# A fused attention and two-MLP kernel: where the last 16 weight blocks are turned from 64-bit words into floats, and the order of a quad's seven products

## The chip, the cores and the metric

The kernel runs on one core of one Trainium2 chip. The metric is the device time of one execution in microseconds (us). Before the change three runs took 874.74, 876.16 and 879.68 us; the median is 876.16 us.

## The reference

All inputs are 64-bit floats, the output is 32-bit. Cut to what matters:

```python
# attention: 4 batches, 8 heads, 576 positions, head size 64, causal window of 64
attn = softmax(masked(q @ k.T / 8)) @ v          # -> x, 2304 tokens x 512
# first MLP
h = (x @ w1) * (x @ w2) @ w3                     # 512 -> 1024 -> 1024
x = h @ w_out                                    # 1024 -> 512
# second MLP
h = x @ w_in                                     # 512 -> 2048
out = maximum(0.01 * h, h) @ w_out2              # 2048 -> 512
```

The weight `moe2_w_out` of the last line is called `w_out2` in the kernel, `moe2_w_in` is `w_in`.

## The kernel before, in words

**Arithmetic.** Each matmul operand is split into a high part (fp32r) and a low part, and `mm3` (lines 74 to 77) adds three matmuls, high x high, high x low and low x high. ACT writes the high part, DVE subtracts to get the low part.

**Words.** A weight arrives as 64-bit words, 128x512 of them (512 KB) to a *unit*. `advance` (line 283) moves a pipeline of units on by one step at each call: one unit is scaled by ACT (line 292), and DVE does three operations per unit, a mask-and-or (line 306), a shift (line 313) and an or (line 317); then `fin` uses the 128x512 float block `f`. A unit passes its stages in four successive calls, and a new call can start the next one. `load_unit` (line 273) issues the load of the raw words on SP into one of four `raw` buffers; `feed` loads ahead as far as the buffers allow. The blocks `f` also have four buffers (tag "f"), and both tags are shared with other uses: `w_ops` takes two `f` and one `raw`, `y_ops` four `f` and two `raw`, `load_w` one `f`.

The first 40 units (w3, w_out, w1, w2) are used at once. The next 32 (16 of `w_in`, 16 of `w_out2`) are only converted and stored as floats into the DRAM tile `wd` (`keep`, line 381), to be read back later. Before the change all 32 are converted beside the first MLP, from batch 2 on: one or two calls of `advance` per step of the loop at line 629 (lines 636 to 638).

**Stages in order of time.** Attention of a batch runs beside the first MLP of the batch before it.
- *x to y*: for each of 4 batches 16 steps (two token halves, eight blocks f). `ab_step` computes two products in PSUM (tag "ab"); ACT copies one of them (line 495), DVE multiplies (line 500) and splits. `y_step`, two steps later, accumulates y in four PSUM banks with w3 @ w_out already multiplied together. y goes to the DRAM tile `yd`.
- *y to h*: 24 *quads*. Each is a 2x2 block product by a seven-product scheme (`class Quad`, line 585): w side p of 0 to 7 (`NF`), token side c of 0 to 2 (`NP`). Each product is six matmuls of 128x384 into a PSUM bank (tag "pr"); there are eight banks, two in the pool `ps_h` and six in `ps2`. ACT copies the first product of a quad (line 606), DVE adds the others to partial sums (line 608, seven adds a quad), and SP stores four results per quad to the DRAM tile `hd`. `w_ops(p)` reads floats of `w_in` back from `wd` and makes seven sums and splits; `y_ops(c, j)` does that for y. For c = 2 the low parts of y are made by GpSimd (POOL) instead of DVE. The quads' order (line 741): p = 0 to 2 for c = 0, 1 and 2 (quads 0 to 8), then p = 3 to 7, each for c = 0 to 2 (quads 9 to 23).
- *h to out*: `o_step`, 6 token blocks x 16 blocks of h. `load_w` and `split_w` bring `w_out2`'s floats from `wd`, `load_h` and `split_h` the blocks of h. `ahead` issues them some steps early; the first four calls stand behind quad 21.

**Order of the work.** A planner replays the program with a model of each instruction's duration and writes a fixed order for each engine. An instruction that was written earlier in the program has priority; `first()` (line 70) lifts what stands in it by 3000 places. `tc.issue_after(ins)` makes the instructions in its block stand behind `ins` on the same engine. On the chip each engine then keeps the planned order, whatever the times turn out to be. The quads' products carry no such tie, so the planner can put a product of a later quad ahead of one of an earlier quad when a `ps_h` bank is free and a `ps2` bank isn't; it can also put quad 0's first two products (in `ps_h`) between the last steps of x to y.

**Loads at the seam.** `early` (line 656) holds `w_ops(0)`, `y_ops(0, 0)` and `y_ops(0, 1)`. The first is called at step 2 of the last batch, the other two only when all 32 units are through (line 639) or behind the loop (lines 657 to 659).

Of the kernel before, what the change touches and what calls it, by code (L numbers as in the profile page):

```python
# [21 lines left out]
def tile_kernel(ctx: ExitStack, tc: tile.TileContext, q, k, v, w1, w2, w3, w_out, w_in, w_out2, out):  # L22
# [16 lines left out]
    B, H, S, D = q.shape  # L39
# [34 lines left out]
    def mm3(ps, lh, ll, rh, rl, first, last):  # L74
        pe.matmul(ps, lhsT=lh, rhs=rh, start=first, stop=False)  # L75
        pe.matmul(ps, lhsT=lh, rhs=rl, start=False, stop=False)  # L76
        return pe.matmul(ps, lhsT=ll, rhs=rh, start=False, stop=last).ins  # L77
# [185 lines left out]
    units = []  # L263
    last = {}
    slots = {}
    n_of = {"load": 0, "scale": 0, "shift": 0, "bits": 0, "fin": 0}

    def feed():

        while n_of["load"] < min(len(units), n_of["bits"] + RAW):  # L270
            load_unit()

    def load_unit():
# [9 lines left out]
    def advance(stop):  # L283

        now = dict(n_of)
        if now["scale"] < min(stop, now["load"]):
            u = units[now["scale"]]
            w = flat(u["raw"]).bitcast(I32).rearrange("p (m two) -> p m two", two=2)
            u["lo"], u["hi"] = w[:, :, 0], w[:, :, 1]
            u["f"] = stage.tile([P, UC], F32, name="f", tag="f", bufs=4)  # L290
            with tc.issue_after(pss["copy"]) if now["scale"] >= PHASE_B else nullcontext():
                act.mul(u["f"], u["hi"].bitcast(F32), 2.0 ** -112)  # L292
                if now["scale"] < PHASE_B:
                    u["low"] = stage.tile([P, UC], I32, name="low", tag="low", bufs=1)
                    act.activation(out=u["low"], in_=flat(u["raw"]).bitcast(U8).rearrange("p (m e) -> p m e", e=8)[:, :, 3],
                                   func=AF.Copy, scale=1.0 / 32, bias=-31.0 / 64)
            n_of["scale"] += 1
        if now["fin"] < now["bits"]:
            u = units[now["fin"]]
            u["fin"](u["f"])  # L300
            n_of["fin"] += 1
        d = now["bits"] < now["shift"]
        if d:
            u = units[now["bits"]]
            f = u["f"].bitcast(I32)
            dve.scalar_tensor_tensor(out=f, in0=u["hi"], scalar=-0x80000000, in1=f, op0=ALU.bitwise_and, op1=ALU.bitwise_or)
        if now["shift"] < now["scale"]:
            u2 = units[now["shift"]]
            g = u2["f"].bitcast(I32)
            if "low" in u2:  # L310
                dve.scalar_tensor_tensor(out=g, in0=g, scalar=3, in1=u2["low"], op0=ALU.logical_shift_left, op1=ALU.bitwise_or)
            else:
                dve.tensor_scalar(g, g, 3, 0x7FFFFFF8, op0=ALU.logical_shift_left, op1=ALU.bitwise_and)
            n_of["shift"] += 1
        if d:
            if "low" not in u:
                dve.scalar_tensor_tensor(out=f, in0=u["lo"], scalar=29, in1=f, op0=ALU.logical_shift_right, op1=ALU.bitwise_or)
            n_of["bits"] += 1
            feed()

    def until(n, stop):
        while n_of["fin"] < n:
            advance(stop)
# [57 lines left out]
    def keep(i):  # L381

        return lambda f: sp.dma_start(wd[i], f)

    for p in range(NF):
        for h in range(2):
            unit(w_in[2 * P * h:2 * P * h + 2 * P, 2 * P * p:2 * P * p + 2 * P].rearrange("(k p) m -> p k m", p=P),
                 keep(2 * p + h), ("win", p, h))
    for f in range(KF2):
        unit(w_out2[P * f:P * f + P, :], keep(KF2 + f), ("wo2", f))  # L390
    KEPT = len(units)
    for name, p in [("wo", i) for i in range(4)] + [(n, p) for p in range(2) for n in ("w1", "w2")] + [("wf", i) for i in range(4)]:
        slots[name, p] = wslot((name, p))

# [112 lines left out]
    def y_step(b, hf, i):  # L507
        w = rows2(slots["wf", i // 2])
        for j in range(KD):
            if i == 0:  # L510
                yps[j] = ps_mm.tile([P, DM], F32, name="mm", tag="mm")
            ws = slice(P * j, P * j + P)
            mm3(yps[j][:, 0:NH], w[:, 0, i % 2, ws], w[:, 1, i % 2, ws], ab[i][:, 0], ab[i][:, 1], i == 0, i == KF - 1)
        if i == KF - 1:
            for j in range(KD):
                y = stage.tile([P, DM], F32, name="io", tag="io", bufs=2)[:, 0:NH]
                t0 = b * S + hf * NH
                with first():
                    act.copy(y, yps[j][:, 0:NH])
                    act.dma_start(yd[:, j, t0:t0 + NH], y)  # L520
# [64 lines left out]
    class Quad:  # L585
# [4 lines left out]
        def product(self, m):  # L590
            n_of["bank"] += 1
            pool = ps_h if n_of["bank"] % 8 in (1, 2) else ps2
            ps = pool.tile([P, DM], F32, name="pr")[:, 0:NB2]
            a, b = PRODUCTS[m]
            w, y = wop[self.p][a], yop[self.c]
            for j in range(2):
                ws = slice(P * j, P * j + P)
                pss["last"] = mm3(ps, w[:, 0, ws], w[:, 1, ws], y[:, b, j, 0], y[:, b, j, 1], j == 0, j == 1)
            return ps

        def add(self, to, ps, of):

            if to not in self.sb:
                self.sb[to] = ph.tile([P, NB2], F32, name="c", tag="c", bufs=8)
            if of is None:
                act.copy(self.sb[to], ps)
            else:
                dve.tensor_tensor(out=self.sb[to], in0=ps, in1=self.sb[of], op=ALU.add)  # L608

        def out(self, n):  # L610
            fh, th = int(n[1]) - 1, int(n[2]) - 1
            t0 = (2 * self.c + th) * NB2
            sp.dma_start(hd[:, 2 * self.p + fh, t0:t0 + NB2], self.sb.pop(n))

        def step(self, k):
            m, adds, done = ((1, [("c11", None)], []), (6, [("c12", "c11")], []), (2, [("c11", "c11")], ["c11"]),
# [9 lines left out]
    for b in range(B):  # L626
        if b + 1 < B:
            plan_att(b + 1, *((10, 26) if b == 0 else (1, 37)))
        for s in range(2 * KF):
            hf, f = divmod(s, KF)  # L630
            if b == 0:
                if hf == 0:
                    until(max(last[n, f // 2] for n in ("w1", "w2")), PHASE_B)
                for _ in range(2):
                    advance(PHASE_B)
            if 2 * KF * b + s >= 2 * KF * (B - 2) + 4:
                for _ in range(2 if b == B - 1 and s < 8 else 1):
                    advance(KEPT)
            if b == B - 1 and (s == 2 or n_of["fin"] == KEPT and len(early) > 0):
                early.pop(0)()  # L640
            ab_step(b, hf, f, 0)
            slot()
            ab_step(b, hf, f, 1)
            slot()
            ysteps.append((b, hf, f))
            if len(ysteps) > YLAG:
                y_step(*ysteps.pop(0))
            slot()
        if b == B - 2:
            att.release()  # L650
            xa.release()
            ps_at.release()
            ps_h = tc.alloc_tile_pool(name="ps_h", bufs=2, space=PSUM, side="right", reuse_waits="tile")
            yb0 = tc.alloc_tile_pool(name="yb0", bufs=1, side="right", reuse_waits="tile")
            yop[0] = yb0.tile([P, 7, 2, 2, NB2], F32R, name="yop")
            early = [lambda: w_ops(0), lambda: y_ops(0, 0), lambda: y_ops(0, 1)]
    until(KEPT, KEPT)
    for f in early:
        f()
    for e in ysteps:  # L660
        y_step(*e)

# [81 lines left out]
    for i, q in enumerate(quads):  # L744
        for k in range(7):
            with first():
                q.step(k)
            if k == 0 and order[i] == (NF - 1, 0):
                for f in range(WLEAD):
                    load_w(f)  # L750
            if k == 0 and i < FIRST * (NP - 1) and i % FIRST == 0:
                c = i // FIRST + 1
                yop[c] = ph.tile([P, 7, 2, 2, NB2], F32R, name=f"yop{c}", bufs=1)
            if k == 3:
                if i == 0:
                    w_ops(2)
                elif i < FIRST * (NP - 1) and i % FIRST in (1, 2):
                    y_ops(i // FIRST + 1, i % FIRST - 1)
                p = order[i][0] + 2 if order[i][1] == NP - 1 else 0
                if FIRST <= p < NF:  # L760
                    w_ops(p)
        if order[i] == (NF - 1, 0):
            yb0.release()
            po1 = tc.alloc_tile_pool(name="po1", bufs=4, side="right", reuse_waits="tile")
            for n in range(LOADS):
                ahead(n)
# [40 lines left out]
```

## Time and profile before

| what | value |
|---|---|
| median of 3 runs | 876.16 us |
| the profiled execution | 876.7 us, of which the span from first to last instruction is 874.9 us |
| PE (matmul) busy | 824.2 us, 94% of the span |
| DVE busy | 572.9 us, 65% |
| ACT busy | 391.0 us, 45% |
| POOL busy | 60.4 us, 7% |
| mean granted TensorE clock | 0.986 of full speed |
| last matmul of x to y ends | about 475.2 us |
| last product of y to h ends | about 663.7 us |
| first matmul of h to out starts | 666.35 us |

PE is busy nearly all the time, so the places of interest are the few where it isn't, and the ones where its clock is at the lower level. Busy shares are averages over stages with different limits; a table by stage is among the rows below.

### The profile page before, as it was taken

How to read it: one execution, taken by the hardware profiler on the slowest of the kernel's cores; microseconds unless marked ns; L12 is line 12 of the kernel's file. 1: busy time of each engine (PE TensorE's matmuls, PEld its weight loads, DVE VectorE, ACT ScalarE, POOL GpSimd, SP SyncE). 2: the span in 40 equal slices, each digit the busy share in tenths (PEclk: the TensorE clock that was granted, in tenths of full speed). 3: DMA queues.
4: the chain of work that ended last, by engine and by line, in shares of the span. 5: the costliest groups of instructions: out<-in, count | busy, mean ns of one | idle time of the engine just before them, and what ended most of it. 6: DMA issues, size and time to landing. Idle time of an engine off the chain costs nothing.

```text
span 874.9 us, 15295 instructions
## 1 busy us (share of the span) xinstructions
PE 824.2 (94%) x5332; PEld 754.2 (86%) x5332; DVE 572.9 (65%) x1435; ACT 391.0 (45%) x988; POOL 60.4 (7%) x75
## 2 busy tenths in 40 slices
PE   4789799999999999999998899999997999999997
PEld 3577699899999999999888899999996888888885
DVE  6799897554555377767775986565658555555552
ACT  6687883433343344435354421111125545555552
POOL 1012011110111011100000340000000000000000
PEclk9999999999999999999999999999998999999999
DMA  7798778763556267877962554343447335344341
GB/s 240 200 214 230 209 188 202 164 148 92 119 122 138 59 171 197 246 239 245 281 204 62 161 184 163 103 154 112 151 152 228 106 93 155 107 135 128 100 127 45
DMA packets 203693, 139.44 MB, mean 159 GB/s; under 512 B 137312, under 2 KB 181856, under 8 KB 203616
## 3 DMA queue, kind: packets, MB, share of 16 engines
q1 hardware_dynamic: 199008, 133.74, 54.3%
q10 hardware_dynamic: 4608, 4.72, 1.6%
q8 instruction: 42, 0.69, 0.3%
q14 instruction: 35, 0.29, 0.1%
HBM read 94.63 MB, written 43.78 MB: 158 GB/s over the span
## 4 chain that ended last, share of the span: by engine, by line
PE 66%; DMA 14%; DVE 11%; ACT 5%; issue 2%; SPq 1%; POOL 0%; ACTq 0%; DVEq 0%; POOLq 0%
PE o L75 8%; PE o L76 8%; PE o L77 8%; PE ab L75 6%; PE ab L76 5%; PE ab L77 5%; PE pr L75 5%; PE pr L76 5%; PE pr L77 5%; DMA raw<-in_moe_w_out_dram 3%; PE mm L75 3%; DMA raw<-in_moe_w_dram 3%; PE mm L77 3%; PE sc L175 2%; PE mm L76 2%
## 5 line engine op out<-in xcount | busy, mean ns | idle before, releaser
L75 PE MATMUL ab<-x,w 128*128 128x288 f32 x512 | 154.5, 302 | 5.2 <-ACT x L235 2.6
L76 PE MATMUL ab<-x,w 128*128 128x288 f32 x512 | 151.9, 297 | 0.0
L77 PE MATMUL ab<-x,w 128*128 128x288 f32 x512 | 151.4, 296 | 0.0
L75 PE MATMUL o<-w,g 128*128 128x512 f32 x288 | 114.5, 397 | 2.7 <-DVE c L608 2.7
L608 DVE TENSOR_TENSOR c<-pr,c 128x384 f32<-128x384 f32 x168 | 84.3, 549 | 46.1 <-PE pr L77 27.4
L76 PE MATMUL o<-w,g 128*128 128x512 f32 x288 | 114.2, 396 | 0.0
L75 PE MATMUL pr<-yop,w 128*128 128x384 f32 x324 | 100.5, 343 | 8.8 <-DVE c L608 6.4
L75 PEld LDWEIGHTS ab<-x,w 128*128 128x128 f32 x512 | 96.8, 189 | 8.1 <-ACT x L235 2.8
L76 PE MATMUL pr<-yop,w 128*128 128x384 f32 x324 | 98.9, 339 | 1.4 <-DVE yop L542 1.4
L76 PEld LDWEIGHTS ab<-x,w 128*128 128x128 f32 x512 | 96.8, 189 | 0.2
L77 PEld LDWEIGHTS ab<-x,w 128*128 128x128 f32 x512 | 96.8, 189 | 0.0
L77 PE MATMUL pr<-yop,w 128*128 128x384 f32 x324 | 96.1, 340 | 0.0
L696 DVE TENSOR_TENSOR t<-h,t 128x384 f32<-128x384 f32 x96 | 53.5, 558 | 50.5 <-ACT t L695 50.5
L77 PE MATMUL o<-w,g 128*128 128x512 f32 x288 | 84.0, 396 | 0.0
L695 ACT ACTIVATE t<-h 128x384 f32<-128x384 f32 x96 | 50.4, 525 | 56.9 <-DVE g L698 56.1
L77 PE MATMUL mm<-ab,wf 128*128 128x288 f32 x256 | 74.8, 295 | 0.0
L75 PE MATMUL mm<-ab,wf 128*128 128x288 f32 x256 | 74.6, 308 | 0.0
L76 PE MATMUL mm<-ab,wf 128*128 128x288 f32 x256 | 74.3, 293 | 0.0
L698 DVE TENSOR_TENSOR g<-t,g 128x384 fp32r<-128x384 f32 x96 | 53.5, 557 | 28.6 <-ACT g L697 28.1
L75 PEld LDWEIGHTS pr<-yop,w 128*128 128x128 f32 x324 | 60.7, 190 | 12.3 <-DVE c L608 9.4
L75 PEld LDWEIGHTS o<-w,g 128*128 128x128 f32 x288 | 54.8, 190 | 15.4 <-issue 3.0
L292 ACT ACTIVATE f<-raw 128x512 f32<-128x512 f32 x72 | 48.6, 677 | 42.3 <-DMA raw<-in_moe_w_out_dram 23.7
(99 smaller groups left out, 1505.7 us busy)
## 6 DMA issues: line engine op xcount, KB each, us to landing
hd<-c SPq DMA_DIRECT2D x96, 192.0 KB, 2.2
h<-hd SPq DMA_DIRECT2D x96, 192.0 KB, 2.4
raw<-in_moe_w_dram SPq DMA_DIRECT2D x32, 512.0 KB, 4.5
raw<-in_moe_w_out_dram SPq DMA_DIRECT2D x24, 512.0 KB, 5.2
raw<-in_moe_w_in_dram SPq DMA_DIRECT2D x16, 512.0 KB, 4.9
wd<-f SPq DMA_DIRECT2D x32, 256.0 KB, 4.6
f<-wd SPq DMA_DIRECT2D x32, 256.0 KB, 3.2
vt<-in_v_dram SPq DMA_DIRECT2D x56, 128.0 KB, 2.7
```

The costliest lines, as they stand in the source:

```text
L75: pe.matmul(ps, lhsT=lh, rhs=rh, start=first, stop=False)
L76: pe.matmul(ps, lhsT=lh, rhs=rl, start=False, stop=False)
L77: return pe.matmul(ps, lhsT=ll, rhs=rh, start=False, stop=last).ins
L175: pe.matmul(sc[:, t, :], lhsT=qb[:, t, :], rhs=kT[n][:, k0:k0 + P], start=True, stop=True)
L292: act.mul(u["f"], u["hi"].bitcast(F32), 2.0 ** -112)
L608: dve.tensor_tensor(out=self.sb[to], in0=ps, in1=self.sb[of], op=ALU.add)
L695: act.mul(t, h, 0.01)
L696: dve.tensor_tensor(out=t, in0=h, in1=t, op=ALU.max)
L698: dve.tensor_tensor(out=g[:, 1], in0=t, in1=f32(g[:, 0]), op=ALU.subtract)
```

## The change: the edits and the diff

- `n_of` gets `cap` and `room`. `feed` loads units only up to `cap`. While x to y runs, `cap` and `KEPT` end behind `w_in`'s 16 units, so `w_out2`'s 16 aren't touched there.
- In the loop of x to y `advance` is called once per step in place of once or twice; `y_ops(0, 0)` and `y_ops(0, 1)` are called at steps 8 and 11 of the last batch. The `until(KEPT, KEPT)` behind the loop goes.
- From quad 6 on, at the second and fifth product of each quad: the first such call raises `cap`, sets `room` to 3 raw buffers and loads; each later one is an `advance`, until all units are through. The scaling on ACT is tied behind the last copy of a quad's first product, the loads on SP behind the last store of a quad's result.
- Each product of a quad is tied behind the product before it on PE, the very first behind the last `y_step`.
- `load_w(0)` to `load_w(2)` are called at the fourth product of quad 20, within `first()`, in place of behind the first product of quad 21.

```diff
-    n_of = {"load": 0, "scale": 0, "shift": 0, "bits": 0, "fin": 0}
+    n_of = {"cap": 0, "room": RAW, "load": 0, "scale": 0, "shift": 0, "bits": 0, "fin": 0}
...
-        while n_of["load"] < min(len(units), n_of["bits"] + RAW):
+        while n_of["load"] < min(n_of["cap"], n_of["bits"] + n_of["room"]):
             load_unit()
...
+    n_of["cap"] = KEPT = len(units)
     for f in range(KF2):
         unit(w_out2[P * f:P * f + P, :], keep(KF2 + f), ("wo2", f))
-    KEPT = len(units)
...
-            mm3(yps[j][:, 0:NH], w[:, 0, i % 2, ws], w[:, 1, i % 2, ws], ab[i][:, 0], ab[i][:, 1], i == 0, i == KF - 1)
+            pss["pr"] = mm3(yps[j][:, 0:NH], w[:, 0, i % 2, ws], w[:, 1, i % 2, ws], ab[i][:, 0], ab[i][:, 1], i == 0, i == KF - 1)
...
-            for j in range(2):
-                ws = slice(P * j, P * j + P)
-                pss["last"] = mm3(ps, w[:, 0, ws], w[:, 1, ws], y[:, b, j, 0], y[:, b, j, 1], j == 0, j == 1)
+            with tc.issue_after(pss["pr"]):
+                for j in range(2):
+                    ws = slice(P * j, P * j + P)
+                    pss["pr"] = mm3(ps, w[:, 0, ws], w[:, 1, ws], y[:, b, j, 0], y[:, b, j, 1], j == 0, j == 1)
...
-                act.copy(self.sb[to], ps)
+                pss["copy"] = act.copy(self.sb[to], ps).ins
...
-            sp.dma_start(hd[:, 2 * self.p + fh, t0:t0 + NB2], self.sb.pop(n))
+            pss["store"] = sp.dma_start(hd[:, 2 * self.p + fh, t0:t0 + NB2], self.sb.pop(n)).ins
...
             if 2 * KF * b + s >= 2 * KF * (B - 2) + 4:
-                for _ in range(2 if b == B - 1 and s < 8 else 1):
-                    advance(KEPT)
-            if b == B - 1 and (s == 2 or n_of["fin"] == KEPT and len(early) > 0):
+                advance(KEPT)
+            if b == B - 1 and s in (2, 8, 11):
                 early.pop(0)()
...
-    until(KEPT, KEPT)
-    for f in early:
-        f()
...
-            if k == 0 and order[i] == (NF - 1, 0):
-                for f in range(WLEAD):
-                    load_w(f)
+            if k == 3 and order[i] == (NF - 2, NP - 1):
+                with first():
+                    for f in range(WLEAD):
+                        load_w(f)
+            if k in (1, 4) and i >= FIRST * (NP - 1) and n_of["fin"] < len(units):
+                if n_of["cap"] == KEPT:
+                    n_of["cap"], n_of["room"] = len(units), 3
+                    feed()
+                else:
+                    advance(len(units))
```

## Rows read from the trace of the kernel before

**Rows 1.** Busy time by stretch: length, busy us (instructions), PEclk, DMA share, GB/s.

```profile
398.00:475.20 77.20, 73.15 (x534) 71.20 (x532) 52.12 (x111) 30.83 (x69) 0.00 (x0) 1.00 0.63 199
475.20:526.20 51.00, 46.09 (x239) 44.63 (x240) 45.52 (x84) 20.27 (x44) 16.15 (x14) 0.93 0.54 168
526.20:599.60 73.40, 72.64 (x415) 72.32 (x415) 44.90 (x94) 12.44 (x25) 0.00 (x0) 1.00 0.39 130
599.60:648.60 49.00, 48.28 (x275) 47.65 (x275) 27.62 (x57) 6.00 (x14) 0.00 (x0) 1.00 0.39 132
648.60:666.30 17.70, 13.00 (x72) 12.04 (x70) 15.28 (x30) 9.81 (x19) 0.00 (x0) 0.98 0.88 281
```

**Rows 2.** PE's waits, 400 to 670 us: us in total, times, longest.

```profile
PE pr L75 <- DVE c L608: 6.4, 6, 2.1
PE pr L76 <- DVE yop L542: 1.4, 1, 1.4
PE ab L75 <- DVE p L500: 1.3, 2, 0.8
PE ab L75 <- ACT a L495: 0.9, 2, 0.5
```

**Rows 3.** PE's timeline, 475 to 668 us, five of its waits: start, us, [idle before].

```profile
477.08 0.44 PE L75 MATMUL pr<-yop,w 128*128 128x384 f32 x1 [1.88 <-ACT w L573]
...
493.61 0.44 PE L75 MATMUL pr<-yop,w 128*128 128x384 f32 x1 [0.83 <-DVE c L608]
...
503.61 0.45 PE L75 MATMUL pr<-yop,w 128*128 128x384 f32 x1 [2.10 <-DVE c L608]
...
658.81 0.45 PE L75 MATMUL pr<-yop,w 128*128 128x384 f32 x1 [1.95 <-DVE c L608]
...
666.35 0.77 PE L75 MATMUL o<-w,g 128*128 128x512 f32 x1 [2.69 <-DVE c L608]
```

**Rows 4.** Busy time of five slices of 5 us, for the clock behind the waits.

```profile
475.00:480.00 5.00, 3.12 (x12) 2.70 (x11) 3.76 (x8) 4.42 (x11) 0.00 (x0) 0.77 0.42 125
480.00:485.00 5.00, 5.00 (x27) 5.00 (x26) 3.53 (x7) 2.67 (x7) 0.00 (x0) 0.89 0.65 193
505.00:510.00 5.00, 5.00 (x22) 5.00 (x21) 4.22 (x9) 1.02 (x2) 2.10 (x2) 0.66 0.97 307
665.00:670.00 5.00, 3.65 (x9) 2.91 (x10) 2.98 (x7) 0.77 (x2) 0.00 (x0) 0.54 0.95 322
670.00:675.00 5.00, 5.00 (x19) 4.03 (x18) 4.55 (x8) 4.09 (x8) 0.00 (x0) 0.77 0.51 162
```

**Rows 5.** Groups by line, whole span: count | busy us, mean ns | idle before.

```profile
L608 DVE TENSOR_TENSOR c<-pr,c 128x384 f32<-128x384 f32 x168 | 84.3, 549 | 46.1 <-PE pr L77 27.4 <-ACT c L606 16.8 <-issue 0.5
L306 DVE SCALAR_TENSOR_TENSOR f<-raw,f 128x512 int32<-128x512 int32 x72 | 49.2, 684 | 0.7
L292 ACT ACTIVATE f<-raw 128x512 f32<-128x512 f32 x72 | 48.6, 677 | 42.3 <-DMA raw<-in_moe_w_out_dram 23.7 <-DMA raw<-in_moe_w_dram 15.0 <-DVE nm L179 1.7
L317 DVE SCALAR_TENSOR_TENSOR f<-raw,f 128x512 int32<-128x512 int32 x32 | 23.7, 741 | 0.1
L313 DVE TENSOR_SCALAR f<-f 128x512 int32<-128x512 int32 x32 | 13.5, 421 | 18.1 <-ACT f L292 17.9
```

**Rows 6.** DVE's timeline, 636 to 644 us.

```profile
640.28 4.06 DVE L608 TENSOR_TENSOR c<-pr,c 128x384 f32<-128x384 f32 x8 [8.00 <-ACT c L606]
```

**Rows 7.** DVE's timeline, 650 to 660 us.

```profile
656.05 0.69 DVE L260 TENSOR_TENSOR w<-f,w 128x512 fp32r<-128x512 f32 x1 [2.11 <-ACT w L259]
```

**Rows 8.** ACT's timeline, 650 to 660 us.

```profile
655.40 0.62 ACT L259 CAST w<-f 128x512 fp32r<-128x512 f32 x1 [2.04 <-DMA f<-wd]
```

**Rows 9.** Instructions on tile f: duration ns min/median/max, first to last start.

```profile
L679 SPq DMA_DIRECT2D f<-wd x16: 319/320/1330, 586.7 to 671.2; - x16
```

**Rows 10.** ACT's waits, 314 to 446 us, where w_in's and w_out2's units are converted.

```profile
ACT f L292 <- DMA raw<-in_moe_w_out_dram: 18.0, 11, 3.5
```

**Rows 11.** The page's DMA issues: count, KB each, us to landing.

```profile
raw<-in_moe_w_out_dram SPq DMA_DIRECT2D x24, 512.0 KB, 5.2
```

## The prediction, made before the changed kernel ran

> **What bounds the kernel now.** I read the busy time by stretch first [rows 1]. PE is the bound: in the two middle stretches of y to h it is busy 72.6 of 73.4 us and 48.3 of 49.0. DVE is the second: 45.5 of 51.0 us in quads 0 to 5, where it splits y and w beside the quads' additions, but 44.9 of 73.4 and 27.6 of 49.0 after that. So work on DVE is nearly free from quad 6 on and dear before it. Then PE's waits [rows 2], which show that between 400 and 670 us PE stood still for DVE's additions (6.4 us), for early products whose y wasn't split yet (1.4 us) and for a and b, held up by conversions (1.3 and 0.9 us). The timeline gives five of these their places [rows 3]: the seam from y to the quads (1.88 us), two in quads 0 to 5 (0.83 and 2.10 us), the last quads (1.95 us) and the first `o` (2.69 us). Last the clock: where PE had stood still it came back at the lower of its two levels, 1.2 in place of 2.4 GHz, for a while [rows 4]. Behind the seam the two slices lose 5 x 0.23 + 5 x 0.11 = 1.7 us, behind the wait at 503.6 us 5 x 0.34 = 1.7 us, and around 666 us 5 x 0.46 + 5 x 0.23 = 3.4 us, of which some 0.3 us fell on the wait itself, so 3.1 us. The wait at 658.8 us has no drop of its own size behind it: the 17.7 us stretch stands at 0.98 [rows 1].
>
> PE's floor in the quads is 72.64 us / 415 = 0.175 us a matmul [rows 1], 1.05 us a product and 7.35 us a quad.
>
> **The change part by part.** I work against the profiled execution, 876.7 us with 1.8 us outside its span of 874.9. It is 0.5 us above the median of 876.16, and that is taken off at the end.
>
> *The 16 units leave x to y.* Each costs DVE 684 + 421 + 741 = 1.85 us and ACT 0.68 us [rows 5], so DVE loses 29.5 us and ACT 10.8 us there. Until 420 us PE is busy without a break, so the relief is worth only what PE waits: for a and b 0.84 us (the longest of two) and twice under 0.5 us, 0.9 together [rows 2]. The other wait for p, 1.3 less 0.84 us, comes where y's splits are in the way and no units are left; I leave it. Gain 1.7 us; bounds 0 and 2.2.
>
> *Quad 0's first two products go behind the last y.* Before, they stand between steps of x to y and wait there for y's splits, 1.4 us [rows 2]. That wait goes; the 12 matmuls (2.1 us) are only moved. Gain 1.4 us, with the same row as its upper bound and 0 as the lower. Nothing is lost in x to y, since PE is full there without them.
>
> *The seam.* Before, the two `ps_h` banks had been used up early, so the next thing in PE's order was the second product of quad 1, which needs `w_ops(1)`; its tiles lie where the first MLP's weights lay, and so it came only 1.88 us after the last y [rows 3], plus 1.7 us of clock [rows 4]: 3.6 us. After, quad 0 runs in order with everything it needs at hand: two products in `ps_h` and two in the banks of a and b, 4 x 1.05 = 4.2 us of work, in which ACT empties the y banks. What is late next is the fifth product, if its bank is one of the last two y banks, which wait for a store buffer. I take 3.0 of 3.6 us, near the top because 4.2 us of cover is more than the 1.88 us that was waited for; lower bound 0, if the additions on DVE merely return it later.
>
> *Quads 0 to 5.* The same 45.5 us of DVE work now meets 252 products' matmuls, 44.1 us of PE. The wait of 2.10 us and its 1.7 us of clock come from a full DVE, not from the order; I keep them. Bounds: 3.8 us gained, or 3 us lost.
>
> *The tie between products.* DVE once stood 8.00 us waiting for the copy of a quad's first product while PE ran later products, and then did ten additions in one go [rows 6]. In order, the copy comes first and additions keep step. Waits of PE in the middle quads are of that kind: of the six behind additions, 6.4 us in total [rows 2], those in quads 0 to 5 and the last quads are 0.83, 2.10 and 1.95 us [rows 3]; 1.5 us are left. Gain 1.5 us; bounds 0 and 1.5, and none lost unless a product blocked by `w_ops` can't be passed any more.
>
> *The 16 units go to quads 6 to 15.* With one call to start the loads and then two steps a quad, 16 units and three steps of lag need 19 calls, so ten quads. DVE would need 44.9 + 29.5 = 74.4 us in a stretch of 73.4 us [rows 1, 5], so it is full; over this stretch and the next it is 102.0 of 122.4 us. Additions stand in `first()` and units don't, so the planner puts units into the holes, and the eight banks cover 8.4 us of delay. `f` has four buffers, of which a `w_ops` takes two, which stretches the units beyond quad 15. SP gets 16 loads and 16 stores more; they stand behind the stores of results by the tie. A load lands in 5.2 us [rows 11], which three loads ahead cover. I put the cost at 2.0 us, by the nearest rows, the waits for DVE in quads 0 to 5 at a like load. Bounds 0, and 18 us (the slower rival below).
>
> *The loads a quad sooner.* Before, the first `wd` load is issued at 586.7 us [rows 9], long before any split of w at 648.6 us, so the first blocks weren't late and sooner loads bring nothing. What is late is a following block: ACT waits 2.04 us for it [rows 8], DVE 2.11 us behind ACT [rows 7], and the additions queued behind that wait make PE's 1.95 us and, as DVE catches up, the 2.69 us before the first `o` [rows 3], with 3.1 us of clock: 7.7 us in all. The later blocks need buffers freed by the first splits, which need quad 21 done; that stays. But in order DVE may enter the last quads with less to catch up; I take 1.2 us of gain, nearer to nothing. Bounds 0 and 7.7.
>
> Sum: 876.7 - 1.7 - 1.4 - 3.0 - 1.5 + 2.0 - 1.2 = 869.9 us, less 0.5 for the median: 869.4, told as 869.
>
> **The rivals.**
> *The end stall goes too (860 us).* If ordered additions leave DVE free when the w blocks come and units cost nothing, the rest of the 7.7 us (6.5) and the 2.0 go: 869.4 - 8.5 = 861, and a little of the 3.8 us in quads 0 to 5 makes 860. For it: DVE is idle 8.00 us before burst work [rows 6]. Against it: the late block hangs on a DMA, which isn't changed.
>
> *DVE takes it back (874 us).* It is nearly full in quads 0 to 5; if PE comes earlier, it waits later. Then the seam's 3.0 us come back and units cost 4.0 us: 869.4 + 3.0 + 2.0 = 874.4, no change. For it: DVE at 45.5 of 51.0 us [rows 1], and PE's 3.6 us at the seam were time that DVE used.
>
> *Slower: a unit's load holds up the additions (885 us).* ACT's scaling waits for the raw words; behind it on ACT are the copies of quads' first products, behind the shift on DVE the additions. In x to y ACT waited 18.0 us in 11 places, up to 3.5 us, for these loads [rows 10], and DVE 17.9 us for ACT [rows 5]. There PE didn't care. In the quads, at a full DVE, the delay can't be made up, and past the eight banks it falls on PE: 869.4 - 2.0 + 18.0 = 885. It decides from the point where over 9 us of the 18 get through. For it: the DMA share would rise from 0.39, with 16 loads of 512 KB [rows 11] and 16 stores of 128x512 floats, 256 KB, together 12.6 MB in 73.4 us, 171 GB/s on top of 130; the stretch with 281 GB/s stands at 0.88, so this one would be at about 0.9 [rows 1]. Against it: three loads ahead, and 21 us of room on DVE behind quad 15.
> Of such a queue the Trainium skill (PSUM — Partial Sum Buffer, section Engine vs sequencer instructions) says that the queues of ScalarE and VectorE are strictly first in, first out. The trace agrees: behind the split that waited 2.11 us until 656.05 us [rows 7] no addition came in time, and PE stood until 658.81 us for one [rows 3]. By that rule every wait of a unit counts in full once DVE has no slack, which is this rival's 885; without it the additions would pass and the time would be 867.
>
> *The change doesn't do what it says* in its last part: the loads were early anyway, which the sum has.
>
> **How the numbers follow.** Chances: my forecast 0.45 (its own range 864 to 874), end stall gone 0.19, taken back 0.21, slower 0.15. What a measurement of this kernel can tell from no change is about 0.5%, 4.4 us: faster is under 871.8, slower over 880.5. Faster: 0.19 + 0.34 of the forecast's 0.45 + 0.05 = 0.58. Slower: 0.15 and 0.02 of the taken-back case = 0.17. Same: 0.25. The range is 857 to 881: below it is the end of the first rival, above it most of the slower one.
>
> **What would show it.** Right: no product matmul between a and b's before 470 us; no PE wait over 1 us at the seam and a clock of 1.00 behind it; additions seven a quad with no DVE wait over 3 us for a copy from quad 6 on; DVE over 90% in quads 6 to 15 with PE over 98%. Wrong: PE waits for additions in quads 6 to 15 that add up to over 4 us, with ACT waiting for `raw` just before them; or a wait before quad 6 for y's splits. The end stall at its old size means no 860; without it the forecast is too high.

## The result, and the profile after

The changed kernel takes 868.43 us (median of eight runs beside as many of the kernel before at 876.52 us). One run of each took over three times as long (3404.53 and 2798.83 us); the ratio of the means of the seven others is 0.9907, with a 95% interval of 0.9882 to 0.9932. The forecast was 869.0 us. The profiled execution took 868.42 us, 866.6 of it span, against 876.7 us before. PE's busy time fell from 824.2 to 820.7 us and the mean clock rose from 0.986 to 0.990.

The stages of the two profiled executions, in us. Twelve matmuls (2.1 us) that stood inside x to y before now stand behind it, which the fourth column takes out:

| stage | before | after | difference, with the 12 matmuls put level | forecast |
|---|---|---|---|---|
| last y ends at | 475.2 | 466.9 | -6.2 | -3.1 |
| seam and quads 0 to 5 | 51.0 | 52.1 | -1.0 | -3.0 |
| quads 6 to 23 | 137.5 | 140.7 | +3.2 | -1.5 + 2.0, and a part of -1.2 |
| from the last product to the first `o` | 2.7 | 0.2 | -2.5 | the rest of -1.2 |
| h to out | 202.1 | 200.4 | -1.7 | |

The same stretches by busy time: length, PE, PEld, DVE, ACT, POOL busy (instructions), PEclk, DMA share, GB/s. These answer to [rows 1]. The quads are cut at 519.0 (quad 6 begins), 578.2 and 615.4, the last lines are the end and h to out, and one slice of 5 us:

```profile
398.00:466.90 68.90, 68.90 (x522) 68.84 (x521) 30.23 (x68) 21.68 (x52) 0.00 (x0) 1.00 0.19 59
466.90:519.00 52.10, 46.73 (x251) 42.88 (x250) 44.62 (x79) 20.54 (x44) 16.07 (x14) 1.00 0.47 154
519.00:578.20 59.20, 59.12 (x338) 58.54 (x338) 50.71 (x105) 15.63 (x29) 0.00 (x0) 1.00 0.82 267
578.20:615.40 37.20, 31.91 (x170) 30.66 (x169) 30.31 (x65) 9.70 (x18) 0.00 (x0) 0.95 0.76 249
615.40:652.00 36.60, 36.60 (x211) 36.60 (x210) 23.52 (x45) 7.17 (x15) 0.00 (x0) 1.00 0.47 155
652.00:659.90 7.90, 7.74 (x46) 7.45 (x44) 7.90 (x17) 4.92 (x11) 0.00 (x0) 1.00 1.00 319
659.90:860.30 200.40, 199.60 (x864) 162.21 (x864) 111.20 (x203) 103.45 (x203) 0.00 (x0) 1.00 0.39 119
...
605.00:610.00 5.00, 4.47 (x17) 4.47 (x18) 4.40 (x11) 2.03 (x4) 0.00 (x0) 0.68 0.83 251
```

The reader is to see three things. In the first line PE is busy for all of 68.90 us, with DVE down to 30.23 from 52.12 us: x to y has no hole left. Only one line has PE short of work late in the quads, 578.2 to 615.4, with 31.91 of 37.20 us. And the end, 13.00 of 17.7 us in [rows 1], is now 7.74 of 7.90.

PE's timeline of the changed kernel, with the waits that count from the seam on (start, us, what it did, idle before); it answers to [rows 3]:

```profile
471.95 0.44 PE L75 MATMUL pr<-yop,w 128*128 128x384 f32 x1 [0.91 <-ACT io L519]
480.97 0.44 PE L75 MATMUL pr<-yop,w 128*128 128x384 f32 x1 [1.02 <-DVE c L609]
...
585.26 0.45 PE L75 MATMUL pr<-yop,w 128*128 128x384 f32 x1 [1.56 <-ACT c L607]
588.08 0.44 PE L75 MATMUL pr<-yop,w 128*128 128x384 f32 x1 [1.47 <-DVE c L609]
605.52 0.44 PE L75 MATMUL pr<-yop,w 128*128 128x384 f32 x1 [2.26 <-DVE c L609]
659.83 0.47 PE L75 MATMUL o<-w,g 128*128 128x512 f32 x1 [0.16 <-ACT w L259]
```

The seam's 1.88 us are 0.91, the 2.10, 1.95 and 2.69 us are gone, six waits of 0.46 to 1.02 us (one of them is shown) stand between 480 and 498 us, and three new waits of 5.29 us in all stand from 585 us on: two in quad 14, one in quad 16. What is late at the first two is read on ACT and then on DVE. ACT's timeline:

```profile
575.23 0.47 ACT L607 COPY c<-pr 128x384 f32<-128x384 f32 x1
582.58 0.66 ACT L292 ACTIVATE f<-raw 128x512 f32<-128x512 f32 x1 [6.88 <-DMA wd<-f]
...
584.74 0.47 ACT L607 COPY c<-pr 128x384 f32<-128x384 f32 x1
```

DVE's timeline in the same microseconds:

```profile
578.90 1.01 DVE L609 TENSOR_TENSOR c<-pr,c 128x384 f32<-128x384 f32 x2
579.84 0.41 DVE L570 TENSOR_TENSOR raw<-f,raw 128x256 f32<-128x256 f32 x1
583.28 0.43 DVE L313 TENSOR_SCALAR f<-f 128x512 int32<-128x512 int32 x1 [3.03 <-ACT f L292]
...
584.73 1.02 DVE L609 TENSOR_TENSOR c<-pr,c 128x384 f32<-128x384 f32 x2
```

ACT's scaling of a unit (L292) stands 6.88 us for an `f` block that is still being stored to `wd`. Behind it in ACT's queue is the copy of the next quad's first product, which comes at 584.74; on DVE no addition runs between 579.91 and 584.73, 4.82 us. PE runs on for a while into the free banks and then waits, at 585.26 for that copy and at 588.08 for an addition. Ahead of the third wait, at 605.52, ACT stands 3.50 us until 600.51 for a block that `w_ops` reads back from `wd`, into the `f` buffers that the units use too, with the copy of quad 16 behind it. Over 505 to 650 us ACT's waits for units are these (us in total, times, longest):

```profile
ACT f L292 <- DMA raw<-in_moe_w_out_dram: 28.1, 8, 5.2
...
ACT f L292 <- DMA wd<-f: 8.7, 2, 6.9
```

So beside 36.8 us of waits for units on ACT stand 5.3 us on PE, plus the clock: the slice from 605 us stands at 0.68, 5 x 0.32 = 1.6 us. That the units cause all of it is shown by e5 below, where they are left out.

The end stall is read on DVE too. In the kernel before, DVE's timeline ahead of [rows 7] has only the splits of w and h; no addition starts between 648.58 and 658.21:

```profile
649.84 1.89 DVE L260 TENSOR_TENSOR w<-f,w 128x512 fp32r<-128x512 f32 x3
651.65 1.16 DVE L696 TENSOR_TENSOR t<-h,t 128x384 f32<-128x384 f32 x2
652.78 1.17 DVE L698 TENSOR_TENSOR g<-t,g 128x384 fp32r<-128x384 f32 x2
...
658.21 1.02 DVE L608 TENSOR_TENSOR c<-pr,c 128x384 f32<-128x384 f32 x2
```

In the changed kernel the same splits and the additions (L609) alternate:

```profile
651.60 0.55 DVE L695 TENSOR_TENSOR g<-t,g 128x384 fp32r<-128x384 f32 x1
652.06 0.55 DVE L609 TENSOR_TENSOR c<-pr,c 128x384 f32<-128x384 f32 x1
652.53 0.55 DVE L695 TENSOR_TENSOR g<-t,g 128x384 fp32r<-128x384 f32 x1
653.00 0.55 DVE L609 TENSOR_TENSOR c<-pr,c 128x384 f32<-128x384 f32 x1
653.46 0.68 DVE L260 TENSOR_TENSOR w<-f,w 128x512 fp32r<-128x512 f32 x1
654.06 0.55 DVE L609 TENSOR_TENSOR c<-pr,c 128x384 f32<-128x384 f32 x1
```

### The profile page after: what moved, and what is told of

It is laid out like the page before. It is cut to its first block, busy times and chain, and to the rows that moved or that the text cites. A ratio compares the mean times of both kernels' runs of the same rounds, so it can differ in the third digit from the quotient of the medians.

```text
span 866.6 us, 15318 instructions
## 1 busy us (share of the span) xinstructions
PE 820.7 (95%) x5332; PEld 750.4 (87%) x5332; DVE 573.3 (66%) x1435; ACT 390.9 (45%) x988; POOL 60.6 (7%) x75
## 5 line engine op out<-in xcount | busy, mean ns | idle before, releaser
L75 PE MATMUL pr<-yop,w 128*128 128x384 f32 x324 | 111.4, 344 | 10.7 <-DVE c L609 8.0
L75 PE MATMUL o<-w,g 128*128 128x512 f32 x288 | 113.3, 393 | 0.9 <-ACT g L694 0.8
L76 PE MATMUL o<-w,g 128*128 128x512 f32 x288 | 113.1, 393 | 0.0
L76 PE MATMUL pr<-yop,w 128*128 128x384 f32 x324 | 109.5, 338 | 0.0
L77 PE MATMUL pr<-yop,w 128*128 128x384 f32 x324 | 109.4, 338 | 0.0
L609 DVE TENSOR_TENSOR c<-pr,c 128x384 f32<-128x384 f32 x168 | 87.5, 551 | 19.0 <-PE pr L77 18.1
L77 PE MATMUL o<-w,g 128*128 128x512 f32 x288 | 82.7, 393 | 0.0
L292 ACT ACTIVATE f<-raw 128x512 f32<-128x512 f32 x72 | 48.8, 677 | 61.0 <-DMA raw<-in_moe_w_out_dram 30.9
L183 ACT ACTIVATE s<-s,nm 128x128 f32<-128x128 f32 x144 | 56.6, 397 | 21.1 <-DVE nm L179 20.2
```

The source lines that it names most:

```text
L183: act.activation(out=s[:, t, :], in_=s[:, t, :], func=AF.Exp, bias=nm[:, t:t + 1], scale=-1.0, accum_out=sm[:, t:t + 1])
```

## The experiments

All ratios are to the kernel before on the same chip, with 95% intervals. The kernel before was timed again beside e1 to e4, beside e5 to e8 and beside e9 to e11; it took 873.58, 873.46 and 875.15 us. One table holds what their profiled executions show, worked out from PE's timeline (us; where quad 0's 12 early matmuls stand inside x to y, 2.1 us are taken from its end and put to the quads, so that the columns are alike):

| kernel | tie | w_out2's units in x to y / quads | last y at | to the first `o` | h to out | ratio |
|---|---|---|---|---|---|---|
| before | no | 16 / 0 | 473.1 | 193.3 | 202.1 | 1 |
| changed | yes | 0 / 16 | 466.9 | 193.0 | 200.4 | 0.9907 |
| changed, again (e11) | yes | 0 / 16 | 467.2 | 186.7 | 200.5 | 0.9888 |
| e3, loads not sooner | yes | 0 / 16 | 466.9 | 190.2 | 200.5 | 0.9890 |
| e1, tie alone | yes | 16 / 0 | 472.3 | 185.2 | 200.9 | 0.9922 |
| e4, tie and loads | yes | 16 / 0 | 472.3 | 183.8 | 200.9 | 0.9934 |
| e2, units alone | no | 0 / 16 | 467.4 | 188.8 | 200.8 | 0.9882 |
| e5, no units | yes | 0 / 0 | 467.0 | 185.5 | 200.7 | 0.9841 |
| e6, slow in x to y | yes | 16 / 0 | 476.7 | 184.1 | 201.2 | 0.9979 |
| e8, the same, no tie | no | 16 / 0 | 478.4 | 193.3 | 201.0 | 1.0059 |
| e7, half | yes | 8 / 8 | 466.7 | 185.3 | 199.4 | 0.9845 |
| e10, half, no tie | no | 8 / 8 | 468.8 | 192.1 | 200.2 | 0.9907 |
| e9, scaling on POOL | yes | 0 / 16 | 467.1 | 186.9 | 201.0 | 0.9866 |

A single execution differs from another of the same kernel: the two profiles of the changed kernel are 6.3 us apart in the quads. Ahead of the change they differ too: the step of y that PE begins at 316.53 us in the kernel before begins at 314.62 in e1, 315.47 in e4, 316.56 in the changed kernel and 317.15 in e2, so a difference of 1 to 2 us in the last y can be scatter. So the table says where time is lost, and the ratios say how much.

**e1: the tie alone,** on the kernel before.

```diff
...
+            with tc.issue_after(pss["pr"]):
                 for j in range(2):
...
-                pss["last"] = mm3(ps, w[:, 0, ws], ...)
+                    pss["pr"] = mm3(ps, w[:, 0, ws], ...)
```

> The kernel before with one edit: the products of the quads tied in order behind the last y (units and loads as before). Theory A (the tie brings the gain: no early products waiting in x to y, 1.4 us; a short seam, 2.7 us; middle waits, 1.5 us; and no stall at the end, 7.7 us, because additions stay in step): about 865 us. Theory L (the end stall went because the first w_out2 blocks are loaded sooner and in first place): the end stall stays, 871 to 873 us. Theory U (the units' move brings the gain): 874 to 877 us.

867.38 us, 0.9922 [0.9899, 0.9945]. The end stall is gone, without sooner loads and without units moved: 185.2 us from the last y to the first `o` in place of 193.3. Two groups of ACT's timeline show that the late block didn't come sooner:

```profile
643.19 2.19 ACT L259 CAST w<-f 128x512 fp32r<-128x512 f32 x4 [5.88 <-PE pr L77]
...
650.89 1.28 ACT L259 CAST w<-f 128x512 fp32r<-128x512 f32 x2 [1.02 <-DMA f<-wd]
```

The fifth split of w starts 7.7 us after the first; in the kernel before it was 6.8 us (648.58 to 655.40). So, with units and loads in their old places, the end stall belonged to the products' order. The gain stops at 0.8% because x to y got no faster: the 0.8 us in the table are less than the 1.9 us that e1 was ahead at 316 us. There PE now waits by itself where quad 0's early products had filled the time; the four of PE's waits in this run, 400 to 670 us, that stand in x to y:

```profile
PE ab L75 <- DVE p L500: 3.5, 4, 2.4
...
PE mm L75 <- ACT io L519: 0.9, 1, 0.9
PE ab L75 <- ACT a L495: 0.7, 1, 0.7
PE mm L76 <- DVE ab L502: 0.2, 1, 0.2
```

**e2: the units alone;** the change without the tie and with the loads in their old place.

```diff
...
-            with tc.issue_after(pss["pr"]):
...
-                    pss["pr"] = mm3(...)
...
+                pss["last"] = mm3(...)
...
+            if k == 0 and order[i] == (NF - 1, 0):
+                for f in range(WLEAD):
+                    load_w(f)
```

> The changed kernel without the tie and with the w_out2 loads where they were: only the units moved. Theory A: x to y gains the waits for a and b (1.7 us) and perhaps the early products' 1.4 us, the seam and the end stay as before, the units cost some 6 us in the quads: 878 to 881 us. Theory L: the same. Theory U: 868 to 871 us.

863.64 us, 0.9882 [0.9861, 0.9903]: as fast as the whole change, where the theory with the dear units had 878 and more, and faster than the 868 to 871 us of theory U. The last y comes 5.7 us sooner than in the kernel before, though quad 0's early products still stand in x to y and this execution was 0.6 us behind at 316 us. The 1.88 us at the seam and the 2.10 us in quads 0 to 5 are there as before; at the end PE waits 0.76 and 1.46 us in place of 1.95 and 2.69, so a part of the end stall went here without the tie. PE never waits for an addition between 505 and 650 us; its one wait there is 0.4 us for w. ACT's waits for units, 505 to 640 us, are no shorter than in the changed kernel:

```profile
ACT f L292 <- DMA raw<-in_moe_w_out_dram: 37.9, 12, 7.6
...
ACT f L292 <- DMA wd<-f: 2.9, 2, 2.2
```

So waits on ACT do not by themselves reach PE. In this kernel DVE leaves holes of up to 6.80 us between additions, and PE passes them in the planner's order; in the tied order one of 4.82 us cost 3 us.

**e3: the change with the loads in their old place.**

```diff
-            if k == 3 and order[i] == (NF - 2, NP - 1):
-                with first():
-                    for f in range(WLEAD):
-                        load_w(f)
+            if k == 0 and order[i] == (NF - 1, 0):
+                for f in range(WLEAD):
+                    load_w(f)
```

> The changed kernel with the first three w_out2 loads back behind the first product of quad 21, not in first place. Theory A: no difference, 868 us, first o within 0.5 us of the last product. Theory L: the end stall of 2.7 us with its clock drop and the wait of 2 us before it return, 874 to 876 us.

864.67 us, 0.9890 [0.9868, 0.9912], with a gap of 0.17 us before the first `o`. The sooner loads bring nothing that can be measured.

**e4: the tie and the sooner loads, with the 32 units in x to y as before.**

```diff
-                advance(KEPT)
+                for _ in range(2 if b == B - 1 and s < 8 else 1):
+                    advance(KEPT)
...
-            if k in (1, 4) and i >= FIRST * (NP - 1) and n_of["fin"] < len(units):
-                ...
```

> The changed kernel with w_out2's units converted in x to y again and the y splits called as before; tie and sooner loads stay. Theory A (units cost more in the quads than they did in x to y): quads 14 to 17 lose their 7 us of waits, x to y gets 2 to 3 us of waits back: 863 to 865 us. Theory U (moving the units is what pays): 872 to 876 us.

867.84 us, 0.9934 [0.9912, 0.9955], between what the two theories gave. The units cost x to y 472.3 - 466.9 = 5.4 us, and without them the quads take 183.8 us. It is e1 with the loads sooner, and not faster than e1: a second time the loads bring nothing.

**e5: the price of the units in the quads,** from the same kernel without them. It leaves out the conversion of `w_out2`, with its loads and stores, and reads `w_in`'s floats in their place.

```diff
-    for f in range(KF2):
-        unit(w_out2[P * f:P * f + P, :], keep(KF2 + f), ("wo2", f))
...
-        sp.dma_start(wraw[f], wd[KF2 + f])
+        sp.dma_start(wraw[f], wd[f])
```

> The changed kernel with w_out2's conversion left out (its blocks are read from w_in's floats in place of its own), so that neither x to y nor the quads convert them. Theory Q (the 16 units cost the changed kernel its waits at quads 14 to 17, by holding up ACT): no PE wait between 510 and 650 us, x to y unchanged, 6 to 8 us less than the changed kernel, about 0.982 of the kernel before. Theory T (it is the tied order itself that costs there): waits of 4 us or more stay between 510 and 650 us and the ratio stays at 0.989.

860.53 us, 0.9841 [0.9812, 0.9871], and no PE wait from 510 to 653 us. Against 0.9907 and 0.9888 for the changed kernel, the 16 units in tied quads, their transfers included, cost 0.5 to 0.7%, 4 to 6 us. The interval of e5 ends below the 0.9882 at which that of the changed kernel begins, and overlaps that of e11 (from 0.9863) by 0.1%.

**e6: all 32 units in x to y, begun sooner, one step of the pipeline per step of the loop.**

```diff
-    n_of["cap"] = KEPT = len(units)
     for f in range(KF2):
         unit(w_out2[P * f:P * f + P, :], keep(KF2 + f), ("wo2", f))
+    n_of["cap"] = KEPT = len(units)
...
-            if 2 * KF * b + s >= 2 * KF * (B - 2) + 4:
+            if 2 * KF * b + s >= 2 * KF * (B - 2) - 12:
```

> The changed kernel with all 32 units converted in x to y, one step of the pipeline per loop step from batch 1 on, so neither two steps at a time nor any unit in the quads; tie and sooner loads stay. Theory P (what the units cost x to y before was their pace, two at a time with y's splits just behind): x to y ends within 1.5 us of the changed kernel's, the quads have no wait between 515 and 650 us, ratio about 0.984. Theory W (units in x to y cost what DVE they take): x to y ends 5 us later as in the kernel with the units back, ratio 0.992.

871.87 us, 0.9979 [0.9955, 1.0003]: no gain over the kernel before, and behind the number of either theory. The quads are as good as in e4 (184.1 us), but the last y comes 9.8 us later than in the changed kernel. PE waits there for a small round trip of attention through DRAM:

```profile
294.54 0.77 PE L229 MATMUL pa<-pts,vt 128*64 128x64 f32 x9 [3.62 <-DMA pts<-pd]
...
339.63 0.57 PE L229 MATMUL pa<-pts,vt 128*64 128x64 f32 x12 [0.94 <-DMA pts<-pd]
...
349.72 0.47 PE L229 MATMUL pa<-pts,vt 128*64 128x64 f32 x9 [1.64 <-DMA pts<-pd]
```

What was late at the first of the three is read on SP:

```profile
283.65 6.48 SPq L151 DMA_DIRECT2D qin<-in_q_dram  x4
290.17 2.43 SPq L216 DMA_DIRECT2D pts<-pd  x4
```

DVE had the block ready at 278.61 us, and its store to `pd`, issued at 281.50, landed in 2.8 us. The loads that bring it back were issued only from 290.17 us on, behind four loads of q that took 6.48 us to issue (the longest of them 3.07 us; the median from 270 to 360 us is 0.49), and landed in 2.3 us. So the wait is mostly one in SP's queue. Why those four took so long isn't shown. Over x to y from 260 us on the DMA share is 0.59; the first line below is e6 (PE busy 208.96 of 216.70 us):

```profile
260.00:476.70 216.70, 208.96 (x1694) 203.63 (x1693) 129.66 (x372) 83.37 (x248) 13.74 (x16) 0.99 0.59 169
```

and the second is the changed kernel (206.90 of 206.90 us, share 0.48):

```profile
260.00:466.90 206.90, 206.90 (x1700) 202.66 (x1699) 115.63 (x344) 79.09 (x239) 13.63 (x16) 1.00 0.48 132
```

**e7: half and half.** Eight of w_out2's units stay in x to y, at one step per loop step, eight go to the quads.

```diff
-    n_of["cap"] = KEPT = len(units)
     for f in range(KF2):
+        if f == 8:
+            n_of["cap"] = KEPT = len(units)
         unit(w_out2[P * f:P * f + P, :], keep(KF2 + f), ("wo2", f))
```

> The changed kernel with the first eight of w_out2's units converted in x to y at one step per loop step and the other eight in quads 6 to 11. Theory Q: the waits at quads 14 to 17 go, x to y keeps its gain since nothing is done two at a time, ratio about 0.984. Theory T: ratio 0.989.

860.25 us, 0.9845 [0.9816, 0.9874]: faster than both kernels, and as fast as e5. Its interval ends below the one of the changed kernel, which begins at 0.9882; that of e11 begins at 0.9863 and overlaps it by 0.1%. A wait of 1.42 us for an addition is left before the first `o`. Its windows, where the changed kernel had 31.91 of 37.20 us:

```profile
519.00:578.20 59.20, 59.20 (x342) 59.20 (x341) 52.93 (x113) 15.17 (x28) 0.00 (x0) 1.00 0.76 258
578.20:615.40 37.20, 37.20 (x215) 37.20 (x214) 23.15 (x43) 7.08 (x14) 0.00 (x0) 1.00 0.41 141
```

**e8: e6 without the tie.**

```diff
...
-            with tc.issue_after(pss["pr"]):
...
-                    pss["pr"] = mm3(...)
...
+                pss["last"] = mm3(...)
```

> The kernel with all units slowly in x to y, without the tie between products. It gives the tie alone, with no unit near the quads. If the tie is what shortens the seam and keeps additions in step (theory A): 3 to 6 us slower than the same kernel with the tie. If the gain behind the tie was the planner's luck with one order (rival): within 2 us of it.

878.55 us, 1.0059 [1.0034, 1.0085], 7 us slower than e6. PE's timeline brings back [rows 3] nearly number by number:

```profile
482.39 0.44 PE L75 MATMUL pr<-yop,w 128*128 128x384 f32 x1 [1.88 <-ACT w L573]
508.74 0.69 PE L75 MATMUL pr<-yop,w 128*128 128x384 f32 x1 [2.09 <-DVE c L608]
664.19 0.45 PE L75 MATMUL pr<-yop,w 128*128 128x384 f32 x1 [2.09 <-DVE c L608]
671.73 0.47 PE L75 MATMUL o<-w,g 128*128 128x512 f32 x1 [2.70 <-DVE c L608]
```

**e9: the units' scaling in the quads on POOL in place of ACT,** else the changed kernel.

```diff
-                act.mul(u["f"], u["hi"].bitcast(F32), 2.0 ** -112)
+                if now["scale"] >= KEPT:
+                    pool.tensor_scalar(u["f"], u["hi"].bitcast(F32), 2.0 ** -112, None, op0=ALU.mult)
...
```

> The changed kernel with the scaling of w_out2's units, in the quads, on POOL instead of ACT; all else, also the buffers and the loads, as in the changed kernel. Theory F (the scaling waits on ACT for words or a free block, and the copy of the next quad's first product queues behind it): with the wait on POOL the copies come on time and PE's waits at quads 14 to 17, 5.3 us and a clock drop, shrink to under 2 us; ratio to the kernel before 0.983 to 0.986. Theory D (DVE's own wait for the scaled block holds the additions up, or DVE is simply full): waits of 4 us or more stay, ratio 0.989 to 0.992.

863.42 us, 0.9866 [0.9838, 0.9893]. The waits moved to POOL's queue, where no copy stands behind them (505 to 650 us):

```profile
POOL f L293 <- DMA raw<-in_moe_w_out_dram: 33.6, 5, 18.5
POOL f L293 <- DMA wd<-f: 12.5, 3, 6.5
```

and PE is full in the stretch where it wasn't:

```profile
578.20:615.40 37.20, 37.20 (x212) 36.58 (x211) 34.90 (x73) 7.17 (x14) 9.63 (x5) 1.00 0.80 261
```

Waits of 46.1 us for loads and stores reach PE nowhere between 505 and 650 us; on ACT 5.3 of 36.8 us did. This is what the Trainium skill (PSUM — Partial Sum Buffer, section Engine vs sequencer instructions) says of ScalarE's queue, that it is strictly first in, first out: what waits in it holds up what stands behind it. By the ratios alone e9 and e11 (0.9888 [0.9863, 0.9913]), timed side by side, can't be told apart; the verdict rests on the waits. Before the first `o` PE waits 1.84 us for an addition in this run.

**e10: e7 without the tie.** The edit is that of e8.

> The half-and-half kernel without the tie between products. If the tie is worth something by itself also where the units don't hurt: 3 us or more slower than half-and-half (0.9845), with quad 1's second product ahead at the seam (1.9 us and a clock drop) and waits at the end. If units in the quads already bring a good order without it: within 1.5 us of it.

867.97 us, 0.9907 [0.9876, 0.9937]: 0.6% behind e7, with 1.88 us at the seam, 2.10 us in quads 0 to 5 and 2.87 us at 656.90 us.

**e11: the changed kernel again,** beside e9 and e10.

> The changed kernel itself, beside the two others on one chip: 0.989 to 0.992 of the kernel before, with the waits at quads 14 to 17 again in its trace.

865.10 us, 0.9888 [0.9863, 0.9913]. PE waits 1.47 us at 584.65 and 1.38 us at 601.23, for the same two products as in the last two of the first profile's three waits; the amount is smaller.

## Why the prediction was right or wrong, point by point

The total was right, and the mechanism in part: the tie's gain in the middle quads, the sooner loads and the late y bank came as forecast, four terms were mis-sized. That the total still fits is luck: two gains that were sized too small (3.1 us in x to y, 5.0 us at the end) covered two costs that were sized too small (some 5 us for the units, 2 us in the seam and quads 0 to 5).

- *"The 16 units leave x to y. Gain 1.7 us; bounds 0 and 2.2":* the step that failed most plainly, since it lies outside its bounds. e4 and the changed kernel differ by 5.4 us in x to y, e2 and the kernel before by 5.7, with the 1.4 us for the early products in it. The 2.2 us were all the waits for a and b that [rows 2] showed, and they bounded nothing. Quad 0's early products had filled part of the holes; with the tie they no longer do, and e1's waits in x to y come to 5.3 us, so "PE is full there without them" was wrong too. Nor was all of it idle time: of the 6.2 us of the first table 4.05 are idle in [rows 1] (73.15 of 77.20 us busy). The rest lies for the most part inside the time that counts as busy, since at 396 us the two executions are only 0.3 us apart. The wait left out for coming "where no units are left" belonged to them as well: the changed kernel has none in that stretch.
- *"Gain 1.4 us" for the early products:* not shown. e1 against before gives 473.1 - 472.3 = 0.8 us, which is less than the scatter; the wait for y's splits is gone there, but new waits for a and b stand in its place.
- *The seam, 3.0 of 3.6 us:* 3.6 became 0.9 with a clock of 1.00, and what is late next is the y bank that was named. But quads 0 to 5 took most of it back: 252 matmuls need 44.1 us at the floor and took 52.1, before the change 240 needed 42.0 and took 51.0, so 8.0 us are lost in place of 9.0. The step that failed is keeping the 2.10 us with its clock and adding nothing: both went, and six waits of 0.5 to 1.0 us (4.3 us) came in their place. "From a full DVE, not from the order" was wrong: a wait of 2.1 us stands there in every kernel without the tie (e2, e8, e10) and in none with it. DVE is busy 44.6 of 52.1 us there. That was the mechanism of the rival "DVE takes it back", at about 1.7 us.
- *The tie, 1.5 us in the middle quads:* right; no such wait is left between 500 and 583 us. (The "ten additions in one go" are eight in [rows 6], which is cut at 644 us, and eleven in the whole trace.)
- *The units in the quads, 2.0 us; bounds 0 and 18:* too small. The first profile shows 7 us (5.3 us of waits, 1.6 us of clock), the ratios of e5 give 4 to 6. The mechanism is that of the slower rival, ACT's scaling ahead of the copies, and its sign is there in part: with ACT standing just before them, 3.0 us of waits fall in quad 14, and the 2.3 us that take them over 4 in quad 16, one behind the stretch that was named. But not the 18 us: 36.8 us of waits on ACT reached PE with one part in seven, in two or three places, in quads 14 and 16. The longest was not for raw words but for an `f` block: the change puts units on four blocks of which `w_ops` takes two, which the prediction named as a delay and not as a price.
- *The sooner loads, nothing:* right (e3, and e4 against e1).
- *The end, 1.2 us of 7.7:* too small. 1.95 + 2.5 + 1.7 = 6.2 us went, the 1.7 us read from one execution of each kernel (e8, with the stall back, took 201.0 us from h to out), as in the rival "the end stall goes too". The argument "the late block hangs on a DMA, which isn't changed" failed: in e1 no load is moved and the stall is gone. A late block held up DVE's splits, but PE waited because no additions stood between those splits; in order, they do, and in e1 a block as late no longer reached PE. The cure isn't complete in every tied kernel: 1.42 us are left before the first `o` in e7 and 1.84 in e9, and behind it PE waits for a split of h, 0.75 us in the changed kernel and 1.30 in e1.

The parts don't add up: 0.8% by the tie (e1) and 1.2% by the units (e2) are together 0.9 to 1.1%. The tie is worth 193.3 - 185.2 = 8.1 us from y to `o` with no unit in the quads, 9.2 us in e6 against e8 and 6.8 us in e7 against e10, each from single executions. With 16 units there it is worth nothing that can be told (188.8 us in e2; 193.0, 186.7 and 190.2 us in three tied executions). The units in the tied order bring back what the tie took away; half of them does not, and so e7 is the better kernel.

What stays open is why e2's order lets PE pass ACT's waits: how full the banks were when each hole began isn't in the trace, and no run tells it. That `f` blocks alone are the shortage in quads 14 to 16 wasn't tried either, by giving the units blocks of their own.

## What to carry to other kernels

Read a stall at the end of a stage by what stands between the waiting instructions on the engine, not only by the transfer that came last: here the order of the products was the cure, and the transfer was left alone. When filler work is moved under a nearly full engine, the price sits in the queue it is put into ahead of the work that the bound engine needs; place a part of it in each stage up to that stage's slack, or put its waits on a queue where nobody stands behind them. And the waits that a trace shows are no upper bound for a relief: other work, that the same change takes away, may have been filling the holes.

## What the runs showed of the hardware

- POOL did the units' scaling (128x512 floats) in 1.75 us on average, ACT in 0.67 us. This group of e9 shows it (busy us, mean ns, idle before):

```profile
L293 POOL TENSOR_SCALAR f<-raw 128x512 f32<-128x512 f32 x16 | 27.8, 1745 | 59.8 <-DMA raw<-in_moe_w_out_dram 33.6 <-DMA wd<-f 12.5 <-DVE f L320 5.6
```

- DVE's mask-and-or and shift in e9's quads took 723 and 463 ns on average, against 685 and 425 ns in the changed kernel. The medians, 680 and 414 ns, are not longer: the mean comes from two of sixteen each (0.91 and 1.14 us, 0.85 and 0.73 us), all four run while POOL was scaling a unit.
- Four loads of q kept SP's queue for 6.48 us in e6, and the short round trip through DRAM whose second half stood behind them came 3.62 us too late for PE.
- PE's granted clock fell to 0.68, a mean of its two levels (1.2 and 2.4 GHz), over the slice behind the wait of 2.26 us. Behind 1.56 and 1.47 us, 3 us apart, it stayed at 1.00, as the slices from 585 to 600 us show, and so it did behind 2.44 us at 424.25 us in e1 (slices from 420 to 430 us).
